# Moving the q, k, v and output projections of a two-layer attention and gated-feed-forward kernel into its gate/up phase as pairs of 64-row tiles

## The chip, the cores and the metric

The kernel runs on one core of one Trainium2 chip. The metric is the device time of one execution in microseconds (us): the median of 6 runs is 1224.02 us (1219.69 to 1227.65). The profile was taken of one execution: its own time is 1222.22 us, and the span from its first to its last instruction is 1220.4 us.

The engines are named as in the profile: PE is the matrix engine, PEld its weight load, DVE the vector engine, ACT the scalar engine, POOL the GpSimd engine, and SP the queue that issues all DMAs of this kernel.

## The reference

A sequence of 2048 tokens with 576 features passes twice through the same pair of sub-layers, each on a layer-normed input and added to its residual. A is a linear attention with 32 heads of 18 features, B a gated feed-forward layer with 4608 hidden features and no activation function.

```python
def _A_ref(x, wqkv, w_phi, wo):                       # x: 1 x 2048 x 576
    q, k, v = split((x @ wqkv))                       # each 32 heads x 18
    pq, pk = q @ w_phi, k @ w_phi                     # per head
    phi_q = concat([softmax(pq), softmax(-pq)])       # 36 features per head
    phi_k = concat([softmax(pk), softmax(-pk)])
    kv = einsum("bhsf,bhsd->bhfd", phi_k, v)          # summed over ALL tokens
    z = einsum("bhsf->bhf", phi_k)
    o = einsum(phi_q, kv) / (einsum(phi_q, z) + 1e-6)
    return o @ wo

def _B_ref(x, w_gate, w_up, w_down):
    return ((x @ w_gate) * (x @ w_up)) @ w_down

x = x + _A_ref(_layernorm(x), ...)
x = x + _B_ref(_layernorm(x), ...)
x = x + _A_ref(_layernorm(x), ...)
x = x + _B_ref(_layernorm(x), ...)
```

Since kv sums over all tokens, no token's attention output can be made before every token's key of that layer is there. That puts a barrier at the start of each layer.

## The kernel before

**Tiling.** Tokens go in 16 tiles of 128; two tiles make one of 8 blocks (256 tokens) of the feed-forward layer. The 576 features are 4.5 times 128, so x transposed (`xT`) and every weight matrix hold 5 slices of 128 rows, of which the last has 64 rows of data and 64 rows of zeros.

**The feed-forward block.** `t_bmain` (L1138 on) runs the blocks one after the other. In the gate/up phase `gu_quad` (matmuls of L1115) makes hidden features in 9 "quads" of 72 matmuls each, 648 matmuls per block. They use the matrix engine as two tiles of 64 rows that work at the same time: one takes the lower 64 partitions of a slice, the other the upper 64, and each writes another bank of PSUM (the matmul result memory of 8 banks). The half slice of 64 rows is then used once by each tile, for gate and for up (`Wr`). Three pairs of banks go round: a pair holds gate and up of 2 x 128 hidden features, ACT copies the gate to `gsb` (L1158) and DVE multiplies it with the up bank into `hT` (L1160). In the down phase `t_down` (L1182 for 512 columns, L1185 for the other 64) makes 144 matmuls per block in full 128-row tiles. Its weights are not resident: `t_wd` (L1090) streams 18 chunks of 288 KB per block from HBM through 4 slots, and a slot's next load is issued when its chunk has been used.

**The attention of a tile.** `proj` (L845) is one half of a projection: 5 matmuls of 288 columns into one bank; a projection of one tile takes two such halves, 10 matmuls. For keys and queries `softmax_front` follows: ACT copies the bank (`psb`, L858), DVE takes maximum and minimum (L861, L866) and subtracts (L880), POOL subtracts (L871), ACT takes exponentials (L888, L890), DVE sums (L895), ACT inverts (L899, L903), POOL scales (L909). The result `dd` lies in one of 4 slots (pool `sm`). `t_v` projects values (`vx`, L925). `kv_ops` (L940) accumulates kv. `t_aout` takes a tile from its query to the residual: `dd` is transposed by DMA into `eT`, multiplied with the block-diagonal kv (`num`, 12 matmuls of L1034), divided (L1041, L1044, L1050) into the tile `o`, transposed by DMA into `oT`, projected with `Wo` and added to x (L1075). Then `t_ln` norms the tile and transposes it by DMA for its block.

**What sets the order.** All of this is written as generators (threads). A planner, `Sched.run`, holds an estimated duration for every operation and repeatedly records the one that can start earliest by its estimate, with a head start for threads of high priority. What it records is a fixed order of instructions for each engine, with semaphore waits; on the chip each engine follows its own list in order, and SP issues DMAs in order too. A PSUM bank is taken from the pool `pb`. While a gate/up phase holds the lock (taken at the start of a block in `t_bmain`, released after its last quad), no other thread gets a bank:

```python
        if self.lock is not None and th is not self.lock and "pb" in names:
            return False
```

So apart from what took its bank earlier, projections, `num` and `kv` come between a block's last gate/up matmul and the next block's first one, in and around the down phase. `policy(b)` lets block b (from the second on) start only when the two tiles of the following block have their attention output added (`pol` = 0).

## Time and profile before

| What | Value |
|---|---|
| Median of 6 runs | 1224.02 us |
| Profiled execution: time, span | 1222.22 us, 1220.4 us |
| Mean granted clock of the matrix engine | 0.975 |
| PE busy, share of span | 1106.8 us, 91% |
| DVE busy | 597.7 us, 49% |
| ACT busy | 391.0 us, 32% |
| POOL busy | 265.1 us, 22% |
| First gate/up matmul of layer 1 | at 130.93 us |
| First gate/up matmul of layer 2 | at 714.28 us |

A busy PE is not a PE at its peak: matmuls overlap, and their ends are modelled. What a matmul costs is read from the distance between the starts of neighbours. A line such as L1115 is a line of the kernel; names before the arrow are written, those after it are read. The stages are found from the starts of the matmuls of L1115 and L1182. In layer 1 the eight gate/up stages (with what follows them up to the first down matmul) and the eight down stages (with what follows them up to the next block) take:

| Block | 1 | 2 | 3 | 4 | 5 | 6 | 7 | 8 |
|---|---|---|---|---|---|---|---|---|
| Layer 1, from first gate/up matmul, us | 41.82 | 41.70 | 38.56 | 42.57 | 40.44 | 40.44 | 40.44 | 40.44 |
| Layer 1, from first down matmul, us | 32.30 | 31.32 | 39.09 | 24.32 | 22.44 | 21.64 | 21.30 | 64.52 |
| Layer 2, from first gate/up matmul, us | 39.15 | 39.89 | 42.69 | 35.48 | 35.48 | 35.48 | 35.48 | 35.48 |
| Layer 2, from first down matmul, us | 32.28 | 33.21 | 31.54 | 21.48 | 20.40 | 21.57 | 20.07 | 26.48 |

The number 64.52 holds the barrier between the layers, and 26.48 the last addition and store.

### The profile page before, as it was taken

How to read it: one execution, taken by the hardware profiler on the slowest of the kernel's cores; microseconds unless marked ns; L12 is line 12 of the kernel's file. 1: busy time of each engine (PE TensorE's matmuls, PEld its weight loads, DVE VectorE, ACT ScalarE, POOL GpSimd, SP SyncE). 2: the span in 40 equal slices, each digit the busy share in tenths (PEclk: the TensorE clock that was granted, in tenths of full speed). 3: DMA queues.
4: the chain of work that ended last, by engine and by line, in shares of the span. 5: the costliest groups of instructions: out<-in, count | busy, mean ns of one | idle time of the engine just before them, and what ended most of it. 6: DMA issues, size and time to landing. Idle time of an engine off the chain costs nothing.

```text
span 1220.4 us, 32751 instructions
## 1 busy us (share of the span) xinstructions
PE 1106.8 (91%) x14806; PEld 829.7 (68%) x14806; DVE 597.7 (49%) x1209; ACT 391.0 (32%) x919; POOL 265.1 (22%) x258
## 2 busy tenths in 40 slices
PE   5775898999999899999999589999999999999997
PEld 4553676868668585858585367685766767768584
DVE  7877557384774434333335665737454222213131
ACT  6663433342433222323233343333331211112120
POOL 5774214142350202020203321504121000000000
PEclk9897899999999999999999799999999999999999
DMA  7582129164481606150514211918437142342505
GB/s 173 108 320 61 21 57 208 23 163 92 89 177 16 186 13 174 14 167 23 160 28 127 68 21 50 215 22 201 83 73 187 49 138 82 106 115 72 160 28 146
DMA packets 182949, 128.60 MB, mean 105 GB/s; under 512 B 101530, under 2 KB 181658, under 8 KB 181658
## 3 DMA queue, kind: packets, MB, share of 16 engines
q1 hardware_dynamic: 182810, 126.51, 41.2%
q8 instruction: 116, 1.90, 0.7%
q14 instruction: 23, 0.19, 0.0%
HBM read 100.59 MB, written 2.36 MB: 84 GB/s over the span
## 4 chain that ended last, share of the span: by engine, by line
PE 71%; DMA 16%; DVE 8%; ACT 3%; POOL 1%; issue 1%; SPq 0%; DVEq 0%
PE ps L1115 47%; DMA wdr<-in_B_w_down_dram 12%; PE ps L1182 11%; PE ps L845 9%; DMA oT<-o 3%; PE ps L1185 1%; PE ps L940 1%; DVE ss L895 1%; POOL dd L909 1%; PE ps L1034 1%; DVE st L790 1%; DVE mxmn L866 1%; DVE mxmn L861 1%; DVE o L1050 1%; DVE x_sb L1075 1%
## 5 line engine op out<-in xcount | busy, mean ns | idle before, releaser
L1115 PE MATMUL ps<-xT,Wu 64*128 64x256 bf16 x4608 | 572.5, 270 | 2.6 <-DVE x_sb L1206 2.3
L1115 PE MATMUL ps<-xT,Wg 64*128 64x256 bf16 x4608 | 572.3, 270 | 1.6 <-ACT xT L826 1.6
L1115 PEld LDWEIGHTS ps<-xT,Wu 64*128 64x128 bf16 x4608 | 433.4, 94 | 31.7 <-DVE x_sb L1206 2.8
L1115 PEld LDWEIGHTS ps<-xT,Wg 64*128 64x128 bf16 x4608 | 430.7, 94 | 33.4 <-issue 2.4
L1160 DVE TENSOR_TENSOR hT<-ps,gsb 128x512 bf16<-128x512 f32 x288 | 199.0, 692 | 342.1 <-ACT gsb L1158 341.7
L1158 ACT CAST gsb<-ps 128x512 bf16<-128x512 f32 x288 | 168.6, 586 | 527.5 <-PE ps L1115 526.6
L1182 PE MATMUL ps<-wdr,hT 128*128 128x512 bf16 x1152 | 306.7, 381 | 29.8 <-DMA wdr<-in_B_w_down_dram 28.9
L1182 PEld LDWEIGHTS ps<-wdr,hT 128*128 128x128 bf16 x1152 | 112.5, 98 | 173.0 <-DMA wdr<-in_B_w_down_dram 55.5
L1185 PE MATMUL ps<-wdr,hT 128*128 128x64 bf16 x1152 | 222.0, 193 | 0.0
L1115 PE MATMUL ps<-xT,Wr 64*128 64x256 bf16 x1152 | 171.9, 271 | 0.0
L909 POOL TENSOR_TENSOR dd<-dd,ss 128x576 bf16<-128x576 bf16 x123 | 141.3, 1172 | 136.6 <-ACT ss L903 136.6
L871 POOL TENSOR_TENSOR dd<-psb,mxmn 128x576 bf16<-128x576 bf16 x62 | 73.0, 1181 | 390.4 <-DVE mxmn L861 390.4
L1185 PEld LDWEIGHTS ps<-wdr,hT 128*128 128x128 bf16 x1152 | 112.9, 98 | 1.3
L895 DVE TENSOR_REDUCE ss<-dd 128x64 f32<-128x1152 bf16 x64 | 85.5, 1343 | 32.0 <-ACT dd L890 31.6
L1206 DVE TENSOR_TENSOR x_sb<-ps,x_sb 128x512 bf16<-128x512 f32 x32 | 21.8, 681 | 131.3 <-PE ps L1185 131.3
L812 POOL TENSOR_SCALAR xln<-x_sb,nmean,rstd 128x576 bf16<-128x576 bf16 x59 | 47.9, 823 | 144.4 <-ACT rstd L808 144.4
L1115 PEld LDWEIGHTS ps<-xT,Wr 64*128 64x128 bf16 x1152 | 68.8, 95 | 7.2
L858 ACT CAST psb<-ps 128x288 bf16<-128x288 f32 x128 | 50.1, 397 | 61.7 <-PE ps L845 61.0
L888 ACT ACTIVATE dd<-dd 128x576 bf16<-128x576 bf16 x64 | 43.6, 681 | 63.7 <-DVE dd L880 63.6
L861 DVE TENSOR_REDUCE mxmn<-psb 128x32 f32<-128x576 bf16 x64 | 47.6, 744 | 25.9 <-ACT psb L858 25.9
L845 PE MATMUL ps<-Wo,oT 128*128 128x288 bf16 x320 | 49.9, 292 | 11.5 <-DMA oT<-o 8.6
L845 PE MATMUL ps<-Wv,xT 128*128 128x288 bf16 x320 | 54.5, 305 | 4.6 <-ACT vx L925 3.5
(71 smaller groups left out, 788.5 us busy)
## 6 DMA issues: line engine op xcount, KB each, us to landing
wdr<-in_B_w_down_dram SPq DMA_DIRECT2D x288, 288.0 KB, 3.4
Wg<-in_B_w_gate_dram SPq DMA_DIRECT2D x4, 1152.0 KB, 11.9
Wu<-in_B_w_up_dram SPq DMA_DIRECT2D x4, 1152.0 KB, 15.0
x_sb<-in_A_x_dram SPq DMA_DIRECT2D x8, 288.0 KB, 3.3
out_dram<-x_sb SPq DMA_DIRECT2D x8, 288.0 KB, 3.0
Wraw<-in_A_wqkv_dram SPq DMA_DIRECT2D x8, 144.0 KB, 3.2
xT<-xln SPq DMA_TRANSPOSE x58, 3.2
Wv<-in_A_wqkv_dram SPq DMA_DIRECT2D x1, 576.0 KB, 4.5
```

Of the source, the lines that this page charges most:

```text
L812: yield ("alt", [(eng, [Op(dur, (lambda e, j=j: e.tensor_scalar(xln[:, sl[j], 0:576], x_sb[:, ss[j], :], nm[:, sl[j]:sl[j] + 1], rstd[:, s ...
L845: ops.append(Op(d_pe(n), (lambda e, lhsT=lhsT, rhs=rhs, k=k: e.matmul(s.ps[:, bank, 0:n], lhsT, rhs, start=(k == 0), stop=(k == 4))), read ...
L858: yield ("ops", "act", [Op(d_actc(288), (lambda e, h=h, bank=bank: e.copy(psb[:, pz, 288 * h:288 * h + 288], s.ps[:, bank, 0:288])), reads ...
L861: ops = [Op(665, (lambda e: e.tensor_reduce(mxmn[:, pz, 0, :], p3, AX.X, ALU.max)), reads=[("psb", pz, 0), ("psb", pz, 1)], writes=[("mx", ...
L871: yield ("alt", [(eng, [Op(dur, (lambda e: e.tensor_tensor(d1, p3, mxb, ALU.subtract)), reads=[("psb", pz, 0), ("psb", pz, 1), ("mx", pz)] ...
L895: Op(1320, (lambda e: e.tensor_reduce(ss[:, sm, :].rearrange("p (b g) -> p b g", b=2), e4, AX.X, ALU.add)), reads=s.ddk(sm, 0) + s.ddk(sm, ...
L909: yield ("alt", [(eng, [Op(dur, (lambda e, ev=ev, rb=rb: e.tensor_tensor(ev, ev, rb, ALU.mult)), reads=s.ddk(sm, br) + [("ss", sm)], write ...
L1115: out.append(Op(54.3, (lambda e, bank=bank, cs=cs, lhsT=lhsT, rhs=rhs, st=st, sp=sp: e.matmul(ps[:, bank, cs], lhsT, rhs, start=st, stop=s ...
L1158: yield ("ops", "act", [Op(540, (lambda e, g=g, gb=gb: e.copy(gsb[:, g, :], ps[:, gb, :])), reads=[("gu", gb)], writes=[("gsb", g)], excl= ...
L1160: yield ("ops", "dve", [Op(625, (lambda e, g=g, ub=ub, p=p: e.tensor_tensor(hT[:, p, :], ps[:, ub, :], gsb[:, g, :], ALU.mult)), reads=[(" ...
L1182: ops.append(Op(d_pe(512), (lambda e, lhsT=lhsT, bank=bank, slot=slot, fi=fi, f=f: e.matmul(ps[:, bank, 0:512], lhsT, s.wdr[:, slot, fi, 0 ...
L1185: ops.append(Op(d_pe(64) + 3, (lambda e, lhsT=lhsT, sl=sl, slot=slot, fi=fi, f=f: e.matmul(ps[:, Z, 64 * sl:64 * sl + 64], lhsT, s.wdr[:, ...
```

## The change

`proj` now makes a whole projection of a tile in one of two forms, and the planner takes the form of the mode in which the matrix engine stands at that moment. The full form is the 10 matmuls of before. The row form is 18 matmuls on two 64-row tiles: the lower tile does slices 0 to 4 into its first bank and then slices 0 to 3 into the other; the upper one does the same with the banks exchanged. The half slice is used once by each tile, so the fifth slice of each weight matrix (`Wq`, `Wk`, `Wv`, `Wo`) and of `Wraw` now holds its 64 rows of data in the lower partitions for columns 0 to 287 and in the upper ones for columns 288 to 575. A tile may write a bank that the other one has written only after the latter's last matmul there has ended: one wait of PE on its own semaphore.

After a gate/up phase has its three pairs, the lock is opened for requests that carry a flag: projections, which take the two free banks together. Queries and output projections of tiles 4 to 15 (`urgent` = 4) may only be projected inside a gate/up phase, or while the next block waits for its input (`in_row`). `num` of these tiles and `kv` wait for the lock to be free. The DMA that transposes `o` is not issued while a down phase is being recorded (`dn_active`). `pol` goes from 0 to 3, with which a block waits for nothing but its own input; `pace` goes from 8 to 3. The tile `o` is gone: the divided output is written to a second slot of `dd`, with one more 64-column DVE copy that fills its last slice.

```diff
@@ _try_acquire @@
-        if self.lock is not None and th is not self.lock and "pb" in names:
+        if self.lock is not None and th is not self.lock and "pb" in names and not (self.open and len(r) > 3 and r[3]):
@@ run @@
+                elif r[0] == "pe2":
+                    ops = r[1 + self.pe_mode]
+                    deps = []
+                    for o in ops:
+                        deps.extend(tr.deps_for("pe", o.reads, o.writes, o.excl, True, o.order))
+                    est = max(self.free_at["pe"], tr.ready_time(deps), th.t_ready)
+                    th.alt = ("ops", "pe", ops)
@@ __init__ @@
-        self.pol = (0, 0)
-        self.pace = (8, 8)
+        self.urgent = 4
+        self.prio0 = (4, 4)
+        self.dn_active = False
+        self.stuck = False
+        self.pol = (3, 3)
+        self.pace = (3, 3)
...
+    def in_row(self):
+        return self.sc.open or self.stuck
@@ t_load @@
-                ((lambda e: e.dma_start(W[0:64, 4, :], src[512:576])), [(key, 0)], 64 * D * 2)], ("ld", name))
+                ((lambda e: e.dma_start(W[0:64, 4, 0:288], src[512:576, 0:288])), [(key, 0)], 32 * D * 2),
+                ((lambda e: e.dma_start(W[64:128, 4, 288:576], src[512:576, 288:576])), [(key, 0)], 32 * D * 2)], ("ld", name))
@@ proj @@
-    def proj(self, st_, c0, n, Wm, km, bank, src=None, keys=None):
+    def proj(self, st_, Wm, km, banks, src=None, keys=None):
         s = self
         tok = slice(128 * st_, 128 * st_ + 128)
...
+        N = 288
+        full = [Op(d_pe(N), (lambda e, k=k, h=h: e.matmul(s.ps[:, banks[h], 0:N], L[:, k, :], Wm[:, k, N * h:N * h + N], start=(k == 0), stop=(k == 4))),
+                   reads=rd, writes=[("pbd", banks[h])], excl=[("pb", banks[h])]) for h in range(2) for k in range(5)]
+
+        def half(u):
+            r = slice(64 * u, 64 * u + 64)
+            out = []
+            for i, h in enumerate((u, 1 - u)):
+                for k in ((0, 1, 2, 3, 4) if i == 0 else (0, 1, 2, 3)):
+                    out.append(Op(61, (lambda e, h=h, k=k, st=(i == 0 and k == 0), sp=(i == 1 and k == 3): e.matmul(
+                        s.ps[:, banks[h], 0:N], L[r, k, :], Wm[r, k, N * h:N * h + N], start=st, stop=sp, skip_group_check=True)),
+                        reads=rd, writes=[("pbd", banks[h]), ("row", banks[h], u)], excl=[("pb", banks[h])], mode=1,
+                        order=[("row", banks[h], 1 - u)] if i == 1 and k == 0 else []))
+            return out
+
+        row = [o for pr in zip(half(0), half(1)) for o in pr]
+        return ("pe2", full, row)
@@ softmax_front @@
-        gots = yield ("acqn", ["pb"], 2)
+        if rowonly:
+            yield ("when", s.in_row)
+        gots = yield ("acqn", ["pb"], 2, True)
         banks = [g_[1] for g_ in gots]
+        yield s.proj(st_, Wm, km, banks)
@@ t_kv @@
+        yield ("when", lambda: s.sc.lock is None)
@@ t_aout @@
+        if st_ >= s.urgent:
+            yield ("when", lambda: s.sc.lock is None)
+        osm = yield ("acq", "sm")
...
+        ops.append(Op(130, (lambda e: e.tensor_copy(o[:, 576:640], o[:, 512:576])), reads=okeys, writes=okeys))
...
+            if st_ >= s.urgent:
+                yield ("when", lambda: not s.dn_active)
+            yield ("dma", s.g_ot[oTb], (lambda e: e.dma_start_transpose(s.oT[:, oTb, :, :], o[:, 0:640])),
...
+        if st_ >= s.urgent:
+            yield ("when", s.in_row)
+        gots = yield ("acqn", ["pb"], 2, True)
+        banks = [g_[1] for g_ in gots]
+        yield s.proj(st_, s.Wo, "Wo", banks, s.oT[:, oTb, :, :], [("oT", oTb)])
@@ t_bmain @@
+            s.stuck = True
             yield ("wait", ("xTB", L, b))
             for ev in policy(b):
                 yield ("wait", ev)
+            s.stuck = False
             yield ("lock",)
...
+                        if len(prs) == 3:
+                            yield ("open",)
...
                     yield ("unlock",)
+                    s.sc.open = False
+                    s.dn_active = True
```

In the order that the planner then writes, 80 projections stand inside gate/up phases in the row form: 4, 8, 8, 8, 8, 8, 6 and 4 in the eight blocks of layer 1 (54), and 4 in each of blocks 1 to 6, 2 in block 7 and none in block 8 of layer 2 (26). The rest, before the first block and in the barrier between the layers, stays in the full form.

## The prediction

> **What bounds the kernel now.** I read the chain that ended last by engine and line, then the same chain in order of time, then busy time by stage, then single releases in the timeline.
>
> ```profile
> PE 71%; DMA 16%; DVE 8%; ACT 3%; POOL 1%; issue 1%; SPq 0%; DVEq 0%
> PE ps L1115 47%; DMA wdr<-in_B_w_down_dram 12%; PE ps L1182 11%; PE ps L845 9%; DMA oT<-o 3%; PE ps L1185 1%; PE ps L940 1%; DVE ss L895 1%; POOL dd L909 1%; PE ps L1034 1%; DVE st L790 1%; DVE mxmn L866 1%; DVE mxmn L861 1%; DVE o L1050 1%; DVE x_sb L1075 1%
> ```
>
> The end is set by PE's own work and by the weight stream of the down phase (12%). The projections (L845) are 9%, waits for transposed outputs (oT) 3%. In order of time:
>
> ```profile
> 458.15 5.06 PE ps L845 x40
> ...
> 485.56 35.48 PE ps L1115 x648
> ```
>
> ```profile
> 1140.56 3.38 DMA wdr<-in_B_w_down_dram
> 1143.98 0.39 PE ps L1182
> 1144.40 0.22 PE ps L1182
> 1144.65 0.22 PE ps L1182
> 1144.89 0.22 PE ps L1182
> 1145.17 3.19 DMA wdr<-in_B_w_down_dram
> 1148.41 0.39 PE ps L1182
> ```
>
> The first fence gives two prices: four projections cost 5.06, so 1.265 us each, and a gate/up phase costs 35.48, without a stall. The second shows the loop of a down phase: a slot is freed, its load takes 3.2 to 3.5 us, its chunk is consumed, and the same slot comes round after 1148.41 - 1143.98 = 4.43 us. PE needs four chunks in that time. The down stages by themselves show what that costs:
>
> ```profile
> 753.43:785.71 32.28, 30.39 (x264) 18.30 (x262) 24.70 (x60) 10.38 (x27) 15.59 (x15) 1.00 0.86 205
> ...
> 990.00:1025.47 35.47, 35.47 (x650) 31.45 (x648) 12.56 (x21) 9.96 (x17) 0.00 (x0) 1.00 0.10 32
> 1025.47:1045.87 20.40, 18.71 (x146) 8.99 (x145) 1.43 (x3) 0.59 (x1) 0.00 (x0) 1.00 0.77 221
> 1138.39:1158.46 20.07, 19.09 (x147) 8.98 (x146) 1.43 (x3) 0.59 (x1) 0.00 (x0) 1.00 0.78 231
> ```
>
> Columns are length, then busy time of PE, PEld, DVE, ACT, POOL, granted clock, DMA share and GB/s. Neighbouring down matmul groups of one feature slice start 0.245 us per pair apart (0.49 for four), so 144 need 17.64 us; the bare down phases take 20.07 to 21.57, mean 20.9. About 3 us of each are weight latency, and that floor stays if everything else leaves the phase. A full one (first row) costs more than its parts too: 17.64 + 7 projections 8.86 + four num at 0.62 = 28.98 against 32.28, since transposes interrupt the stream and PE waits for oT.
>
> **The price of a row-form projection.** No row shows one, so I build it. The gate/up matmuls are the nearest:
>
> ```profile
> 520.76 0.27 PE L1115 MATMUL ps<-xT,Wu 64*128 64x256 bf16 x1
> 520.77 0.27 PE L1115 MATMUL ps<-xT,Wg 64*128 64x256 bf16 x1
> ...
> 520.97 0.54 PE L845 MATMUL ps<-Wk,xT 128*128 128x288 bf16 x3
> 521.10 0.59 ACT L1158 CAST gsb<-ps 128x512 bf16<-128x512 f32 x1 [0.29 <-PE ps L1115]
> ```
>
> Two tiles start 3 to 4 ns apart and pairs follow each other every 109 ns for 256 columns, 106.7 of them streaming. At 288 columns that is 122.5 ns, and nine pairs are 1.10 us against 1.265: a tenth saved. But each tile enters the bank that the other has just left, and the wait for it (L870 of the new code, `order`) stands directly behind the matmul it waits for. In gate/up the same kind of wait (288 in the kernel) lies ten pairs behind its matmul and costs nothing. Here it costs the whole latency: a matmul of 269 ns plus 13 for 32 more columns, 45 ns from its end to the semaphore in this mode (the last gate/up matmul starts at 520.77 and ACT starts 0.33 later; after a full-tile matmul that step is 14 ns), and 46 ns from a semaphore to the start of the PE work waiting for it (ACT's copy to oT ends at 118.19, the Wo matmul that waits for it starts at 118.25, 9 ns of it before the semaphore). That is 373 ns from start to start where 119 would be normal: 0.25 us per projection. So a row projection is 1.10 + 0.25 = 1.36 us, **0.09 more than the full form**, and 80 of them cost +7.5 us rather than saving 13. Lower bound of the wait: 0, if another tile's work could pass it, which PE's fixed order excludes; 0.22 with the 14 ns. Upper: 0.30.
>
> Here the Trainium skill speaks against the change. "TensorEngine Tiling (Array Packing)", Restrictions and Gotchas, PSUM pressure, says that two row tiles cannot use the same bank at once and that software has to synchronize. The wait therefore can't be left out. "TensorE: Matmul & The Clock Gate", the cost of a per-tile semaphore tail, gives 25 + 4.7 per tile + 26.3 per increment, so 87 ns for two tiles with two increments, where the trace has 45. By that figure the wait is 0.30 and 80 of them cost 3.4 us more. I use the trace.
>
> Behind the waiting matmul stand the rest of both halves and the next quad; ACT's gate copy and DVE's multiply wait for that quad, and they are early by the time it comes.
>
> **The blocks, one by one.** Layer 1 before is 714.28 - 130.93 = 583.4 us, layer 2 1220.4 - 714.28 = 506.1. After, in layer 1:
> - Blocks 2 to 6 hold 8 row projections, two num and kv each. Gate/up 35.48 + 8 x 1.36 = 46.4. Down: the four before that had only kv beside the stream (24.32 less 1.27 for one projection, 22.44, 21.64, 21.30) average 22.2; one num stands ahead of the first down matmul (+0.62), the other is partly covered by weight waits (+0.3). 23.1; sum 69.5, five times 347.5.
> - Block 1: 35.48 + 4 x 1.36 + two num 1.24 + four mode switches at 0.1 (202 ns from a gate/up start to the next full matmul, 109 without a switch) + 3.3 of cold clock, which it has now, = 45.9; down 20.9 + 0.8 = 21.7. 67.6.
> - Block 7: 35.48 + 6 x 1.36 + 22.2 = 65.8. Block 8: 35.48 + 4 x 1.36 + the barrier's 64.5 = 105.4.
> - Sum 586.3: **+2.9**.
>
> Layer 2: block 1 likewise 43.1 (0.5 of stall as now, no cold clock) + 21.7; blocks 2 to 6 35.48 + 5.44 + 20.9 + 0.9 = 62.7, five times 313.6; block 7 35.48 + 2.72 + 20.9 = 59.1; block 8 as now 62.0. Sum 499.5: **-6.6**. The gain there is that of blocks 1 to 3, whose interrupted down phases go; in layer 1 eight projections per block eat it.
>
> **Queues.** SP: in the new order the oT transposes stand behind the 17th weight load of a block, xT and eT behind the 18th. oT is issued when a down phase has about 1 us left and lands 3.1 (median) to 5 us later, before the first Wo, which has two quads (7.9 us) ahead of it. The last weights of a phase find no transpose among them. DVE: I walked a block of layer 1 through its new DVE and ACT order with the durations of the groups (444 to 448 for the halves, 744, 1343, 692 for hT, 586 for the gate copy). Each hT of a quad's first pair has to end about 1.1 us into the next quad, and the tightest place (sum, maximum, minimums of the second query) leaves 0.28 us. The second key's softmax reaches POOL's end 9.7 us after its projection, and PE comes to kv after about 9.6. So the walk finds no stall, but little room. In the trace, gate/up phases in the clear with 3 to 8 us of other DVE work lose 0 to 0.47 us; after, about 190 us of such work lies there, and at their rate (0.65 us in 44) that is **+3**. Without that cover (0.5 us in each quad with a projection, about 60 quads) it would be +30.
>
> **Edits at about nothing.** The fill copy of 64 columns: 59 ns (smallest memset) to 216 ns (the 64-column addition), on a DVE that idles 5 us in a down phase. Memsets keep 288 words per partition; Wraw's 679 ns goes. Four more DMAs and two more half copies at start: their engines wait there for others; uncovered they are under 2 us. Values now take two banks at once before the first block; keys and values alternate in two pairs of banks, and DVE (98 of the first 131 us) stays ahead: 0, between -3 and +5.
>
> Sum: 1220.4 + 2.9 - 6.6 + 3 = 1219.7 in span. The profiled execution is 1.8 over its span and the median 1.8 over that: **1223 us**.
>
> **Rivals.**
> - **The down phase gets cleaner than any now** (20.1, the best bare one, in 14 phases: -11; start -3; stalls 0: -3; the wait at 0.22: -3). For it: no transpose in the stream. Against: the bare ones of layer 2 have none either and vary by 1.5. About 1200.
> - **DVE becomes the bound of the gate/up phase** and the kernel is slower. Place: an hT behind a sum or a subtraction of softmax. It decides from 0.28 us of lateness, after which PE stalls one for one. For it: planned durations are below traced ones (625 for 692, 370 for 448). Against: the walk. At half the uncovered price +15, at the full one +30: 1238 to 1253, say 1243.
> - **The change doesn't do what it says**: the tiles don't overlap with 288 columns, 80 x 1.0 = +80, 1303. The gate/up starts 3 ns apart speak against it.
>
> **How the numbers follow.** About the same: 0.48, own range 1210 to 1236; in it 0.14 falls below 1217.9 and 0.10 above 1230.1 (0.5% either way, what a measurement of this kernel can tell from no change). Cleaner: 0.22, all faster. DVE-bound: 0.28, and 0.02 for no overlap, all slower. Faster 0.36, same 0.24, slower 0.40. The range leaves out half of the cleaner case's lower half and the worst of the slower ones: 1195 to 1250.
>
> **What would show it.** Row projections: 18 starts in about 1.1 us with one hole of 0.37 from start to start in the middle. Gate/up stages of 46.4 in layer 1 and 40.9 in layer 2; down stages near 23 and 22 with the weight loads still 3.4. hT: its wait by PE near zero, or else the second rival. Wrong would be: holes under 0.3, down phases near 20 or over 24, Wo waiting for oT, or a first gate/up matmul outside 128 to 136.

## The result and the profile after

The changed kernel takes 1217.13 us (median of 17 runs, 1213.47 to 1219.99) where the kernel before, run beside it, takes 1224.36 (38 runs). The ratio is 0.9939, with a 95% interval of 0.9925 to 0.9953: faster by 0.6%. The forecast was 1223, so a gain of a tenth of a per cent where six tenths came. Its profiled execution takes 1217.99 us, 1216.2 of it span; before it was 1222.22 and 1220.4.

The chain that ended last, from the page of the changed kernel. In its lines L1170 is gate/up, L1243 and L1246 are down, L878 is a projection in row form, L870 one in full form:

```profile
PE 73%; DMA 15%; DVE 6%; ACT 3%; POOL 1%; issue 1%; SPq 0%; DVEq 0%; POOLq 0%
PE ps L1170 45%; DMA wdr<-in_B_w_down_dram 14%; PE ps L1243 12%; PE ps L878 9%; PE ps L870 3%; DVE ss L935 2%; PE ps L1082 2%; PE ps L1246 1%; PE ps L982 1%; POOL dd L949 1%; DVE dd L920 1%; DVE mxmn L906 1%; DVE mxmn L901 1%; ACT dd L928 1%; ACT dd L930 1%
```

The projections hold 9% in row form and 3% in full form, where they held 9% before. The wait of TensorE for outputs transposed by DMA (oT, 3% before) is gone. The weight stream has *grown*, from 12% to 14%. That is the outline of the result: the projections left the down phase, and what they had covered there came into view (the run with small slots in the kernel before, below, tests that).

The stages show it. Four stretches of the changed kernel, a gate/up and a down phase of layer 1 (block 3) and of layer 2 (block 2). The columns are length, then busy time of PE, PEld, DVE, ACT and POOL, granted clock, DMA share and GB/s:

```profile
264.07:311.12 47.05, 46.33 (x807) 38.49 (x805) 30.40 (x59) 20.47 (x50) 13.81 (x14) 1.00 0.25 51
311.12:333.87 22.75, 20.76 (x181) 10.78 (x178) 7.64 (x20) 1.97 (x5) 3.14 (x3) 1.00 0.72 209
...
779.52:821.68 42.16, 41.49 (x734) 35.28 (x733) 23.42 (x43) 15.62 (x34) 8.48 (x8) 1.00 0.32 57
821.68:842.45 20.77, 19.59 (x160) 9.57 (x156) 4.07 (x14) 0.06 (x1) 0.00 (x0) 1.00 0.77 224
```

A down phase that has lost its projections still takes 20 to 23 us, because 17.64 us of down matmuls stand beside weights that come too late. Summed over a kernel, the move is a wash. By the stage boundaries of the two traces, gate/up phases (16) grew by 68.7 us, from 625.5 to 694.2, and the seven down phases of each layer that aren't its last shrank by 66.0, from 373.0 to 307.0. If I count everything from the first gate/up matmul to the end, the blocks take 1089.5 us before and 1091.4 after (1086.8 in a second execution of the changed kernel, so 2 us are within its swing). All of the gain lies ahead of the blocks: the first gate/up matmul starts at 124.81 instead of 130.93.

### The profile page after: what moved, and what is told of

It reads as the page before. It is cut to its first block, busy times and chain, and to the rows that moved or that the text cites. A ratio compares the mean times of both kernels' runs of the same rounds, so it can differ in the third digit from the quotient of the medians.

```text
span 1216.2 us, 34014 instructions
## 1 busy us (share of the span) xinstructions
PE 1115.5 (92%) x15446; PEld 817.4 (67%) x15446; DVE 612.6 (50%) x1243; ACT 380.2 (31%) x917; POOL 264.7 (22%) x258
## 4 chain that ended last, share of the span: by engine, by line
PE 73%; DMA 15%; DVE 6%; ACT 3%; POOL 1%; issue 1%; SPq 0%; DVEq 0%; POOLq 0%
PE ps L1170 45%; DMA wdr<-in_B_w_down_dram 14%; PE ps L1243 12%; PE ps L878 9%; PE ps L870 3%; DVE ss L935 2%; PE ps L1082 2%; PE ps L1246 1%; PE ps L982 1%; POOL dd L949 1%; DVE dd L920 1%; DVE mxmn L906 1%; DVE mxmn L901 1%; ACT dd L928 1%; ACT dd L930 1%
## 5 line engine op out<-in xcount | busy, mean ns | idle before, releaser
L1170 PE MATMUL ps<-xT,Wg 64*128 64x256 bf16 x4608 | 585.4, 270 | 1.6 <-ACT xT L852 1.6
L1170 PE MATMUL ps<-xT,Wu 64*128 64x256 bf16 x4608 | 583.8, 270 | 1.5 <-DVE hT L1221 1.5
L1170 PEld LDWEIGHTS ps<-xT,Wg 64*128 64x128 bf16 x4608 | 432.4, 94 | 36.4 <-issue 3.3
L1170 PEld LDWEIGHTS ps<-xT,Wu 64*128 64x128 bf16 x4608 | 432.8, 94 | 29.8 <-DVE hT L1221 2.9
L1243 PE MATMUL ps<-wdr,hT 128*128 128x512 bf16 x1152 | 306.2, 382 | 29.2 <-DMA wdr<-in_B_w_down_dram 27.0
L1243 PEld LDWEIGHTS ps<-wdr,hT 128*128 128x128 bf16 x1152 | 112.7, 98 | 182.1 <-DMA wdr<-in_B_w_down_dram 63.4
L1246 PE MATMUL ps<-wdr,hT 128*128 128x64 bf16 x1152 | 222.4, 193 | 0.0
L1170 PE MATMUL ps<-xT,Wr 64*128 64x256 bf16 x1152 | 161.0, 271 | 0.0
L1246 PEld LDWEIGHTS ps<-wdr,hT 128*128 128x128 bf16 x1152 | 113.2, 98 | 0.0
L935 DVE TENSOR_REDUCE ss<-dd 128x64 f32<-128x1152 bf16 x64 | 86.1, 1347 | 24.8 <-ACT dd L930 24.7
L1170 PEld LDWEIGHTS ps<-xT,Wr 64*128 64x128 bf16 x1152 | 59.2, 95 | 7.1
L898 ACT CAST psb<-ps 128x288 bf16<-128x288 f32 x128 | 46.7, 400 | 31.4 <-PE ps L878 16.0
L906 DVE TENSOR_REDUCE mxmn<-ps 128x16 f32<-128x288 f32 x128 | 52.0, 449 | 0.1
L920 DVE TENSOR_TENSOR dd<-ps,mxmn 128x288 bf16<-128x288 f32 x128 | 51.8, 448 | 0.0
```

The lines of the kernel that those rows point to most:

```text
L906: ops.append(Op(370, (lambda e, h=h, pv=pv: e.tensor_reduce(mxmn[:, pz, 1, 16 * h:16 * h + 16], pv, AX.X, ALU.min)), reads=[("pbd", bank)] ...
L920: ops.append(Op(370, (lambda e, d2h=d2h, pv=pv, mnbh=mnbh: e.tensor_tensor(d2h, pv, mnbh, ALU.subtract)), reads=[("pbd", bank), ("mn", pz, ...
L935: Op(1320, (lambda e: e.tensor_reduce(ss[:, sm, :].rearrange("p (b g) -> p b g", b=2), e4, AX.X, ALU.add)), reads=s.ddk(sm, 0) + s.ddk(sm, ...
L1170: out.append(Op(54.3, (lambda e, bank=bank, cs=cs, lhsT=lhsT, rhs=rhs, st=st, sp=sp: e.matmul(ps[:, bank, cs], lhsT, rhs, start=st, stop=s ...
L1243: ops.append(Op(d_pe(512), (lambda e, lhsT=lhsT, bank=bank, slot=slot, fi=fi, f=f: e.matmul(ps[:, bank, 0:512], lhsT, s.wdr[:, slot, fi, 0 ...
L1246: ops.append(Op(d_pe(64) + 3, (lambda e, lhsT=lhsT, sl=sl, slot=slot, fi=fi, f=f: e.matmul(ps[:, Z, 64 * sl:64 * sl + 64], lhsT, s.wdr[:, ...
```

## Experiments

Times are compared by their ratio to the kernel before, which ran beside each. "Start" is the first gate/up matmul in the profiled execution, "blocks" what follows it up to the end of the span; both are read from one execution each, and by the two pairs of the same kernel below "blocks" vary by some 5 us.

| kernel | median us | ratio to before, 95% interval | start | blocks |
|---|---|---|---|---|
| before (first profile) | 1224.36 | 1 | 130.9 | 1089.5 |
| changed | 1217.13 | 0.9939 (0.9925 to 0.9953) | 124.8 | 1091.4 |
| changed, again | 1212.83 | 0.9937 (0.9912 to 0.9962) | 124.8 | 1086.8 |
| before, values in two banks | 1219.90 | 0.9964 (0.9946 to 0.9982) | 128.2 | 1091.8 |
| changed, values one bank at a time | 1227.39 | 1.0017 (1.0002 to 1.0032) | 135.3 | 1090.6 |
| changed, full form | 1217.28 | 0.9932 (0.9911 to 0.9954) | 123.1 | 1092.6 |
| changed, halves apart | 1199.01 | 0.9785 (0.9761 to 0.9808) | 122.4 | 1073.1 |
| changed, small weight slots | 1189.86 | 0.9752 (0.9725 to 0.9780) | 123.3 | 1065.1 |
| the same, again | 1194.85 | 0.9740 (0.9715 to 0.9766) | 122.9 | 1070.0 |
| before, small slots | 1206.14 | 0.9890 (0.9863 to 0.9916) | 133.7 | 1072.4 |
| before, small slots, values in two banks | 1205.58 | 0.9827 (0.9801 to 0.9853) | 129.6 | 1074.7 |
| changed, small slots, full form | 1200.33 | 0.9778 (0.9752 to 0.9803) | 123.9 | 1075.7 |
| changed, halves apart and small slots | 1167.68 | 0.9572 (0.9541 to 0.9602) | 123.2 | 1044.0 |

### Where the shorter start comes from

My theory after the traces was the value projection of layer 1. Before, it took one PSUM bank, issued 5 matmuls, waited for a bank again and issued the other 5. After, it takes two banks and issues all 10. One run adds only that to the kernel before (lines left out are marked by dots):

```diff
+        if L == 1:
+            gots = yield ("acqn", ["pb"], 2)
+            banks = [g_[1] for g_ in gots]
+            yield ("ops", "pe", s.proj(st_, 0, 288, s.Wv, "Wv", banks[0]) + s.proj(st_, 288, 288, s.Wv, "Wv", banks[1]))
...
```

> The kernel before with only this added: in layer 1 a value projection takes its two PSUM banks together and issues its 10 matmuls as one group; everything else stays. Theory (this alone makes the start shorter): first gate/up matmul near 125 us instead of 131, time about 1218 us, and the move of the projections is then worth nothing. Rival (the gain comes out of the move): first gate/up matmul near 131 us, time 1224 us.

The other undoes only that in the changed kernel:

```diff
-        gots = yield ("acqn", ["pb"], 2, True)
-        banks = [g_[1] for g_ in gots]
-        yield s.proj(st_, s.Wv, "Wv", banks)
+        if L == 1:
+            banks = []
+        else:
+            gots = yield ("acqn", ["pb"], 2, True)
+            banks = [g_[1] for g_ in gots]
+            yield s.proj(st_, s.Wv, "Wv", banks)
         for h in range(2):
+            if L == 1:
+                (_, b1), = yield ("acqn", ["pb"], 1)
+                banks.append(b1)
+                yield ("ops", "pe", s.proj(st_, s.Wv, "Wv", (b1, b1))[1][5 * h:5 * h + 5])
```

> The changed kernel with only this undone: in layer 1 the value projection takes one PSUM bank at a time again, its halves of 5 matmuls each with its own bank, as before the change. Theory (the start became 6 us shorter because both halves of a value projection are now issued at once, out of two banks): the first gate/up matmul comes back to about 130 us and the time is about 1223 us. Rival (the start is shorter for another reason, the order of num or the free slots for the soft maximum): first gate/up matmul stays near 125 us, time 1217 us.

Without any move, the kernel before gains 0.36% (4.4 us), and the interval of its ratio just overlaps that of the whole change. With the move but without the pair of banks, the changed kernel is slower than before, 1.0017. Both runs have blocks of 1090 to 1092 us, like before and after. So whether the changed kernel is faster at all hangs on how the value projection takes its banks, and the move that the change is named for shows no gain in the blocks.

What TensorE waits for shows a part of the mechanism. The fences have the value and the kv matmuls between 40 and 120 us (columns: count, busy us, mean ns, then idle time of TensorE just before the group and who ended it; line numbers differ from kernel to kernel). First the kernel before, then the kernel before with values in two banks:

```profile
L845 PE MATMUL ps<-Wv,xT 128*128 128x288 bf16 x125 | 22.2, 315 | 4.1 <-ACT vx L925 3.0 <-DVE dd L880 0.7 <-ACT WT L743 0.4
...
L940 PE MATMUL ps<-vx,dd 128*128 128x152 bf16 (+1 forms) x130 | 11.2, 239 | 14.8 <-POOL dd L909 10.5 <-DVE dd L909 4.3
```

```profile
L845 PE MATMUL ps<-Wv,xT 128*128 128x288 bf16 x120 | 18.3, 299 | 3.5 <-DVE dd L880 3.5
...
L947 PE MATMUL ps<-vx,dd 128*128 128x152 bf16 (+1 forms) x130 | 10.6, 230 | 12.9 <-POOL dd L909 9.2 <-DVE mxmn L866 2.7 <-DVE dd L909 1.0
```

Then the changed kernel with values one bank at a time, and the changed kernel itself:

```profile
L870 PE MATMUL ps<-Wv,xT 128*128 128x288 bf16 x125 | 22.3, 317 | 2.8 <-ACT vx L974 2.5 <-DVE dd L920 0.2
...
L989 PE MATMUL ps<-vx,dd 128*128 128x152 bf16 (+1 forms) x140 | 13.2, 250 | 12.9 <-POOL dd L949 9.9 <-DVE mxmn L906 2.7
```

```profile
L870 PE MATMUL ps<-Wv,xT 128*128 128x288 bf16 x120 | 19.2, 312 | 2.5 <-DVE dd L920 2.5
...
L982 PE MATMUL ps<-vx,dd 128*128 128x152 bf16 (+1 forms) x140 | 11.8, 233 | 5.4 <-DVE mxmn L906 2.9 <-POOL dd L949 1.8 <-DVE dd L949 0.6
```

With one bank at a time, values wait 3.0 and 2.5 us in all for ScalarE to empty the bank of their first half, and in TensorE's fixed order everything behind stands still with them. With two banks that wait is gone in both kernels. The larger wait, that of kv for the features from GpSimd, does not follow from it alone: it is 10.5 us before, still 9.2 with the pair of banks, 9.9 in the changed kernel without the pair, and 1.8 only where the pair and the rest of the change come together. Only there is VectorE busy for nearly the whole window from 80 to 100 us: for 19.91 us, against 15.67 before (16.84 and 14.80 in the two test kernels). That window in the kernel before and then in the changed one, in the columns of the stages above:

```profile
80.00:100.00 20.00, 13.71 (x123) 10.50 (x122) 15.67 (x23) 10.88 (x32) 11.84 (x10) 0.93 0.77 305
```

```profile
80.00:100.00 20.00, 15.75 (x143) 11.24 (x141) 19.91 (x35) 13.47 (x37) 14.98 (x13) 0.96 0.84 335
```

The size is not fully explained. The pair of banks brings the kernel before from 130.9 to 128.2, and (below, with small slots) from 133.7 to 129.6, while its absence sets the changed kernel back by 10.5. The rest of the change without the pair makes the start 4.4 us longer (135.3); with the pair it makes it 3.4 shorter than the pair alone does. The gain lies ahead of the last kv matmul, which starts at 107.0 us before and at 98.9 after (102.5 and 107.7 in the two test kernels); from there to the first gate/up matmul the changed kernel even takes 2 us more, 25.9 against 23.9. Which of its other edits has to come together with the pair, no run separates.

### What the row form is worth

In this run the projections stay where the change puts them, but always in the full form of 10 matmuls:

```diff
-                    ops = r[1 + self.pe_mode]
+                    ops = r[1]
```

> Every projection keeps its new place inside the gate/up phase but is issued in the full-array form of 10 matmuls. Theory (the form is worth little: 1.265 us plus two changes of tiling at about 0.1 us against 1.366 us for the row form): + 0.09 us x 80 = about +7 us, so about 1224 us, the time of the kernel before. Rival (the row form is what the gain comes from, by its 9 pairs at 122 ns): much slower, since the full form would then cost more than 0.2 us more each, 1233 us or above. Rival (the row form with its hole is dearer than the full form with its two switches): 1217 us or below.

From the timeline of this run, an output projection between two gate/up groups:

```profile
199.63 0.27 PE L1170 MATMUL ps<-xT,Wu 64*128 64x256 bf16 x1
...
199.84 1.40 PE L870 MATMUL ps<-Wo,oT 128*128 128x288 bf16 x10
...
201.17 0.28 PE L1170 MATMUL ps<-xT,Wg 64*128 64x256 bf16 x1
```

From the last gate/up start to the next one is 1.533 us by the unrounded starts; less the 0.106 of a normal pair that is 1.427: the 1.265 of a bare full projection and 0.16 for two changes of tiling, which I had at 0.1 each. The row form takes 1.367 by the same reading, so that it saves 0.06 us. That holds for the 70 projections that stand between gate/up groups. The other ten stand beside the num group at the end of a gate/up phase, where the full form needs no changes of its own and is 0.14 us the cheaper (this stretch with two projections takes 3.57 us in the changed kernel and 3.28 in the full form with small slots). By these prices the row form should be worth 70 x 0.06 - 10 x 0.14 = 2.8 us.

The whole time is 0.9932, within 0.1% of the changed kernel: the expected 7 us did not come. By the stage borders the gate/up phases grew by 7 us (701.3 against 694.2), but 3.5 of these are none: in this trace (and in those of three others, values in two banks, values one bank at a time, halves apart) the record of the first down matmul of every phase is missing, which puts each border 0.22 us too late and makes the down phase look as much shorter. What is left, 3.6 us, is about what the down phases differ by between the two executions of the changed kernel (3 us). The run left the value of the form open, so I repeated it where the swing is smaller, with the small weight slots of an experiment further down:

> The changed kernel with 8 small weight slots, and every projection in the full-array form at its new place. The stages of the run with the full form gave 1.427 us a projection inside the gate/up phase (two changes of tiling included) against 1.367 us for the row form, yet the whole time did not differ. Theory (the 0.06 us x 80 = 4.8 us were lost in the swing of the down phases, which small slots take away): about 5 us slower than the changed kernel with small slots. Rival (something gives the 4.8 us back): no slower than that kernel.

> The changed kernel with 8 small weight slots once more, as the measure beside the other two of this call. Ratio to before 0.975 again by every theory.

There the full form takes 1200.33 against 1194.85, 0.9778 against 0.9740: 5.5 us slower. The gate/up phases hold 3.7 of that; the rest lies in the last block of layer 1 and the start, and nothing here shows that it comes from the form. That 5.5 is so near to the 4.8 expected is luck in part, since 80 x 0.06 overlooks the ten places where the full form is cheaper. So the row form is worth 3 to 5 us. Without its wait it would save 1.427 - 1.102 = 0.325 us at each of the 70 places, some 23 us (an estimate, with the 1.102 of the next experiment).

### The hole in the middle of a row projection

Most of what the form could save goes into a wait that it brings along. The timeline of the changed kernel around one output projection:

```profile
203.29 0.57 PEld L878 LDWEIGHTS ps<-Wo,oT 64*128 64x128 bf16 x10
...
203.40 1.53 PE L878 MATMUL ps<-Wo,oT 64*128 64x288 bf16 x18
...
204.26 0.36 PEld L878 LDWEIGHTS ps<-Wo,oT 64*128 64x128 bf16 x8 [0.40 <-PE ps L878]
...
204.77 0.27 PE L1170 MATMUL ps<-xT,Wg 64*128 64x256 bf16 x1
```

Ten matmuls, then the weight load of the eleventh idles 0.40 us for TensorE's own earlier result (the two tiles exchange their banks there), then eight. By the unrounded starts the sixth pair begins 0.37 us behind the fifth, as predicted, where other pairs are 0.12 apart. From the last gate/up start to the next is 1.473 us in row after row of the trace, so 1.367 for the projection. The test puts another group into the hole. It makes the second half a request of its own, which is held back until the planner has given TensorE one more group (pe_groups counts them), in nearly all places 20 gate/up matmuls. The counter and the head start of the second half (the 350.0) in the planner are left out here:

```diff
...
-        return ("pe2", full, row)
+        mode = yield ("pe2", full, row[0:10])
+        if mode:
+            n0 = s.sc.pe_groups
+            yield ("when", lambda: s.sc.pe_groups > n0 or s.sc.lock is None)
+            yield ("ops", "pe", row[10:18], 350.0)
...
```

> The second half of a row projection (8 matmuls) is planned as a group of its own, with one gate/up group (20 matmuls) between the halves; 62 of the 80 row projections get it, about 10 others fall back to the full form beside num at the end of the gate/up phase. Theory (the 0.25 us hole of each row projection is TensorE waiting for its own first half, and nothing else fills it): the hole closes wherever a group stands between, 62 x 0.25 = 15 us, so about 1202 us, and a gate/up phase of layer 1 blocks 3 to 6 of about 45.6 instead of 47.05 us. Rival (VectorE's hT products, which have about 0.28 us of slack a quad, are late as soon as the holes close, or the halves cost a hole each): the time stays at 1215 to 1220 us and stalls on VectorE show in the gate/up phase.

The two halves of an output projection in the timeline of this run:

```profile
196.65 0.78 PE L882 MATMUL ps<-Wo,oT 64*128 64x288 bf16 x10
...
198.35 0.65 PE L882 MATMUL ps<-Wo,oT 64*128 64x288 bf16 x8
```

1199.01 us, ratio 0.9785: 19 us below the changed kernel, for an edit of a few lines. The two halves now take 0.612 and 0.490 us out of the gate/up phase, 1.102 together, so the hole was 0.265 us. 63 projections got it, which is 16.7 us, and ten fell back to the full form beside num, where it is 0.14 us cheaper; against that, five num groups of 0.62 moved into gate/up phases from down phases. That makes 15.0 us less in the gate/up phases, and with the border set right they are 14.7 us shorter. The rest of the 19 is start and down phases. The stalls that the rival expected on VectorE didn't come: TensorE waits 1.5 us for hT in all, as in the changed kernel. A gate/up phase of layer 1 takes 46.27, which looks longer than the 45.6 expected, but a second num of 0.62 us stands in it, and 0.22 is the missing record at its border.

### The weight stream of the down phase

```diff
-CH = 2
+CH = 1
-        self.NPS, self.NSM, self.NVX, self.NET, self.NXP, self.NWD, self.NG, self.NO, self.NOT = 2, 4, 2, 2, 2, 4, 2, 1, 2
+        self.NPS, self.NSM, self.NVX, self.NET, self.NXP, self.NWD, self.NG, self.NO, self.NOT = 2, 4, 2, 2, 2, 8, 2, 1, 2
```

The same bytes and the same memory, in slots of half the size. First in the changed kernel:

> The changed kernel with the down weights in 8 slots of one f tile (144 KB) instead of 4 slots of two (288 KB): same memory, same bytes, twice as many loads. Theory (a down phase with little beside it is held by the time from the release of a slot to the landing of its next weights: 3.4 us of load + 0.98 us of use + the waits = 4.43 us for 4 slots, where TensorE needs 3.92): with 8 slots the loop is about 3.3 + 0.49 + 0.05 = 3.84 us for 3.92 us of TensorE, so the stream no longer holds it; a down phase of layer 2 falls from about 21.3 to 18.5 us, one of layer 1 from about 21.9 to 20, in all about -30 us: 1187 us. Rival (the loads are held by what the queue and its 16 engines can move, or each load costs the same however small): down phases stay at 21 us, time 1217 us or more.

Groups of the down matmuls and their weight loads (the wait for the stream stands last), and the row of the DMA issues, first of the changed kernel and then of this one:

```profile
L1243 PE MATMUL ps<-wdr,hT 128*128 128x512 bf16 x1152 | 306.2, 382 | 29.2 <-DMA wdr<-in_B_w_down_dram 27.0
...
L1243 PEld LDWEIGHTS ps<-wdr,hT 128*128 128x128 bf16 x1152 | 112.7, 98 | 182.1 <-DMA wdr<-in_B_w_down_dram 63.4
...
wdr<-in_B_w_down_dram SPq DMA_DIRECT2D x288, 288.0 KB, 3.4
```

```profile
L1243 PE MATMUL ps<-wdr,hT 128*128 128x512 bf16 x1152 | 297.5, 382 | 10.8 <-DMA wdr<-in_B_w_down_dram 9.9
...
L1243 PEld LDWEIGHTS ps<-wdr,hT 128*128 128x128 bf16 x1152 | 112.9, 98 | 152.4 <-DMA wdr<-in_B_w_down_dram 26.8
...
wdr<-in_B_w_down_dram SPq DMA_DIRECT2D x576, 144.0 KB, 3.1
```

A load of half the bytes lands after 3.1 us instead of 3.4, with up to eight under way instead of four, so most of its time doesn't depend on the size. The wait of TensorE's weight loads for the stream falls from 63.4 to 26.8 us. The ratio is 0.9752, 0.9740 the second time, against 0.9937 of the changed kernel beside it: 23 us, of the 30 expected. Two of its down phases, layer 1 and layer 2:

```profile
304.67:325.44 20.77, 19.75 (x180) 10.87 (x177) 7.63 (x20) 1.97 (x5) 3.15 (x3) 1.00 0.78 228
...
868.26:887.75 19.49, 19.09 (x161) 9.62 (x158) 4.08 (x14) 0.06 (x1) 0.00 (x0) 1.00 0.82 236
```

Blocks 2 to 6 of layer 1 are at 20.0 to 20.9, as expected (20.0 to 21.7 in the second execution); those of layer 2 are at 19.1 to 19.6 (19.8 to 20.0), and not at 18.5: in the chain single loads take 3.6 us there, and a loop of 3.84 against 3.92 us has no room for them. The Trainium skill, "Perfetto Trace Analysis", DMA Optimizations, gives both sides of this: larger transfers use the memory better, and splitting may let some of the work start sooner where the engines have time. Here the DMA share in a down phase was 0.72 to 0.77, and splitting decides.

The same edit in the kernel before asks what its projections in the down phase had been worth:

> The same edit in the kernel before. Theory (projections that stood in the down phase filled the stream's holes there, so a down phase that had them gains little, and the eight with only kv or nothing gain 2.5 us each): -20 us, about 1204 us, so that after this edit the move of the projections is worth some 15 us. Rival (the filled down phases had the same holes): -35 us and more, about 1188 us, and the move stays worth nothing beyond the shorter start.

1206.14, ratio 0.9890, so 13 us and not 20. The eight down phases with little in them went from 173.2 to 157.6 us in sum, 15.6 less. The six that hold projections went from 199.7 to 204.9: they gained nothing, which is what the theory says, and lost 5 besides (4.0 together with their gate/up phases, since the planner also moved work between the two). The start is 2.8 longer. So in the kernel before the projections did fill the holes of the stream. Then the move must be worth something once the holes are gone, which is to be seen when the start is alike:

> The kernel before with two edits that are not the move: layer 1's value projection out of two banks at once, and 8 weight slots of one f tile. It is what the changed kernel with 8 small slots is to be compared with, if the move alone is meant. Theory (with the stream out of the way a projection in the down phase costs its full time there, so that the move is now worth what the stages show, down phases -82 us against gate/up phases +70 us): 12 us slower than the changed kernel with small slots, ratio to before about 0.985. Rival (the difference of those two was the start alone): within 4 us of it, ratio 0.975 to 0.979.

Against 0.9740 it has 0.9827, 10.7 us slower than the changed kernel with small slots. The total is near the 12 expected, but it is not what I took it for: 6.6 of it is the start again (129.6 against 122.9, which the pair of banks alone doesn't bring), and 4.7 is the blocks. By stages, the down phases are 79.0 us shorter and the gate/up phases 71.5 longer. So without holes in the stream the move is worth some 4 to 7 us by these readings (an estimate: 10.7 less 6.6, 4.7 by the blocks, 7.5 by the stages). The two executions of the changed kernel with small slots have blocks of 1065.1 and 1070.0, so the stages alone would not show it.

### Both holes closed

> The changed kernel with both edits: second half of a row projection behind a gate/up group, and down weights in 9 slots of one f tile. Theory (the two holes are independent: one in the gate/up phase, one in the down phase): the gains add, -18 us measured for the first and -30 us expected for the second, about 1169 us. Rival (a shorter gate/up phase brings the loads closer to each other, or VectorE and ScalarE become the bound of the shorter block): less than 35 us in all, 1182 us or more.

With nine small slots (one more than above) and the halves apart: 1167.68 us where the kernel before takes 1219.49 beside it, 0.9572 (0.9541 to 0.9602). The gains add, though what the ninth slot is worth was not tested: 45 us against the changed kernel, where each alone brought 19 and 23. Neither edit is part of the change; this is the fastest kernel that was run.

### What varies by itself

> The changed kernel once more, unaltered, to see what varies by itself: the first gate/up matmul (124.8 us) and the first down phase of layer 1 (25.9 us, of which 2.4 us are a wait of num for the transposed eT). Theory (the wait of num there is a matter of that one execution, and the start varies by 2 us): time 1217 us, first down phase 21 to 24 us. Rival (it belongs to the order): 25.9 us again.

The start came out at 124.78 (124.81 the first time), so it doesn't swing by 2 us as I had supposed, and the first down phase at 25.26 (25.93). That phase was expected at 21.7, and its excess of 4 us belongs to the order. More than a third of the excess comes from the granted clock. Matmul time, granted clock, DMA share and GB/s of the changed kernel in the middle of that phase:

```profile
174.00:177.00 3.00, 2.45 (x20) 1.00 0.97 209
177.00:180.00 3.00, 0.80 (x12) 1.00 0.70 216
180.00:181.00 1.00, 0.99 (x7) 0.76 1.09 388
181.00:182.00 1.00, 1.00 (x7) 0.50 0.22 73
182.00:183.00 1.00, 1.00 (x7) 0.50 0.24 18
183.00:184.00 1.00, 1.00 (x7) 0.53 0.86 265
184.00:185.00 1.00, 1.00 (x11) 1.00 0.37 70
```

A weight load with a transpose of eT beside it takes 4.90 us there instead of 3.4 (that the transpose is what delays it is argued, not tested), and TensorE has only twelve num matmuls in the 4.9 us up to 180.0. Then the clock falls to half for about 3.4 us (7 matmuls in a microsecond where there are 11), which costs 1.7 us more. The second execution has the same at the same place. In the kernels with small slots, with the halves apart or with single value banks this phase takes 20.9 to 21.8 us; with the full form 22.7 and 23.3.

## Why the prediction came out as it did

The measured time lies within the range of the forecast, and in its likeliest case, that nothing much happens. By parts, against the span of the changed kernel:

| part | predicted us | measured us |
|---|---|---|
| start, to the first gate/up matmul | 130.9 | 124.8 |
| layer 1, block 1 | 67.6 | 70.7 |
| layer 1, blocks 2 to 6 | 347.5 | 345.2 |
| layer 1, block 7 | 65.8 | 65.8 |
| layer 1, block 8 | 105.4 | 106.4 |
| layer 2, block 1 | 64.8 | 66.6 |
| layer 2, blocks 2 to 6 | 313.6 | 318.0 |
| layer 2, block 7 | 59.1 | 58.1 |
| layer 2, block 8 | 62.0 | 60.6 |
| stalls on VectorE | 3 | in the blocks |
| span | 1219.7 | 1216.2 |

- **The price of a row projection** was right: 1.36 predicted, 1.367 measured, and the reason was right: the hole is 0.37 us from start to start, as forecast, and it closes when other work stands in it. The figure of the Trainium skill, "TensorE: Matmul & The Clock Gate", the cost of a per-tile semaphore tail, would have made it 1.40; the measurement decides for the 45 ns of the trace.
- **The comparison with the full form** was mis-sized. I set 1.36 against a full form of 1.265, so that the form cost 7.5 us. Between gate/up groups the full form costs 1.427, and there the row form saves 0.06. Against the kernel before this makes no difference, since its projections stood mostly in the down phase and paid no change of tiling.
- **The gate/up phase of layer 1** was right: 47.05 less the num of 0.62 that stands at its end is 46.43, predicted 46.4. Layer 2 has 42.16 less 0.62, 41.54, predicted 40.9. Of the 0.6, 0.47 (from start to start) is one stall of TensorE on hT in each of five blocks, 2.4 us in all, which I had in the sum as 3 for stalls. It stands behind a sum of the softmax (L935), where the rival placed it; the timeline of the changed kernel:

```profile
812.17 1.35 DVE L935 TENSOR_REDUCE ss<-dd 128x64 f32<-128x1152 bf16 x1 [1.32 <-ACT dd L930]
...
813.44 1.28 DVE L1221 TENSOR_TENSOR hT<-ps,gsb 128x512 bf16<-128x512 f32 x2
...
813.60 0.27 PE L1170 MATMUL ps<-xT,Wg 64*128 64x256 bf16 x1
...
814.18 0.28 PE L1170 MATMUL ps<-xT,Wu 64*128 64x256 bf16 x1 [0.31 <-DVE hT L1221]
```

  That rival never decided. With the halves apart, quads come closer together still, and TensorE's idle time for hT stays at 1.5 us in all, 0.31 in each of five blocks.
- **The floor of the down phase** was right: 21.5 to 22.8 us in blocks 2 to 6 of layer 1 and 20.8 to 22.3 in layer 2, near "23 and 22" less the num ahead of it, with loads at 3.4. The experiments with small slots confirm its cause. The rival "cleaner than any now" fell.
- **Block 1 of layer 1** was under-sized by 3.1 (gate/up 44.8 where 45.9 was predicted, down 25.9 for 21.7): a late weight load beside a transpose of eT, and the clock after the wait. I had written that the last weights of a phase find no transpose among them, and did not ask about the first ones.
- **The start** is the step that failed. I had listed "values now take two banks at once" among the edits at about nothing, since VectorE "stays ahead", and gave it -3 to +5. It was -6.1, outside that range and outside the 128 to 136 that I had named as a sign of error. VectorE was busy for only 15 to 16 of 20 us between 60 and 100 us, and I didn't ask what its idle time waited for. TensorE's waits would have told a part: values on a copy of ScalarE, 3.0 us. Taking two banks is worth 2.7 us in the kernel before and 10.5 in the changed one; why it is worth more there stays open.

So the blocks were predicted at 1088.8 with the stalls and took 1091.4, the start at 130.9 and took 124.8. That the sum came within 3.5 us is luck in part: the start was 6.1 too long and the blocks 2.6 too short, and the 2.6 is itself a sum of errors of both signs. That the blocks would hardly change was forecast for reasons that the stages bear out. That the kernel became faster was given 0.36, and it came through a part that the forecast held for neutral.

## What to carry to other kernels

Moving work out of a phase that waits for a stream gains little if the work was filling the waits; first find what the wait is (here the landing time of loads into too few, too large slots), close it, and then ask where the work should stand. A wait of an engine for its own last result costs its whole latency when nothing stands between (0.265 us here), and putting independent work there is worth more than a cheaper form of the same work. And an edit that looks neutral, like taking two buffers at once, should be priced where the engine order is fixed, since whatever it waits for holds all that is queued behind it.

## What the hardware showed beyond what I expected

- The granted clock falls to half not only after an idle stretch but after a thin one: 4.9 us with 0.8 us of matmul in them, then 3.4 us at half. "TensorE: Matmul & The Clock Gate", Part 1, of the Trainium skill has a window of about 3.4 us and half rate after an idle one; this trace agrees on the length, and adds that a dozen small matmuls inside do not keep the clock. A wait of 2.2 us for weights thus cost nearly 4.
- In each of the 13 traces all changes of the granted clock fall on one grid of 3.41 us, so the clock can be read against the matmul time of each window of the grid (its ends are modelled). The window ahead of the drop above, 177.1 to 180.5, holds 1.25 us, 1.18 in the second execution. Over all traces the 119 full-rate windows that were followed by a drop held at most 2.02 us, and the 4159 that were followed by full rate at least 1.44: under 1.44 us of matmul the next window always went slow, over 2.02 it never did.
- Two changes between row tiles and the full array cost 0.16 us together (1.427 less 1.265), in rows that repeat to 2 ns.
- A load of 144 KB (eight slots) lands after 3.1 us and one of 288 KB (four slots) after 3.4, at some 210 to 240 GB/s in all; by these two, about 2.8 us don't depend on the size (an estimate: 3.1 less the 0.3 that the second half adds).
